# A step's output rows, four to a partition: the output product's stationary operand taken at every fourth column

## The chip, the cores and the metric

The kernel runs on one core of a Trainium2 chip. The metric is the device time of one execution, in microseconds; three executions of the kernel before are given, and one more was profiled. Five engines of the core appear below: PE does matmuls (PEld is its loading of the stationary operand, shown apart), DVE, ACT and POOL do elementwise work, SP issues transfers. ACT issues transfers as well; a q behind an engine's name (ACTq, SPq) means its queue of such issues.

## What is computed

A channel attention is followed by a gated convolution, for 4 batches of 6,336 rows and 256 channels:

```python
qn = q / (np.linalg.norm(q, axis=1, keepdims=True) + 1e-06)
kn = k / (np.linalg.norm(k, axis=1, keepdims=True) + 1e-06)
s = kn.transpose(0, 2, 1) @ qn / tau            # 256 x 256 per batch
a = softmax(s, axis=-1)
x = v @ a                                       # 6336 x 256 per batch
gate = sigmoid(causal convolution of x over 5 rows, one filter per channel)
out = (gate * (x @ w_val)) @ w_out
```

All inputs and the output are float32, apart from the three weights, which come as float64.

## The kernel before

The scores `s` need all rows of a batch, so a batch has two phases, and the second phase of one batch runs beside the first of the next. In the first, `score_group` takes three rows per partition of q and k, splits part of them into a high and a low half (`hi` holds both) and multiplies them on PE into `s_ps` (L235). There the stationary operand is dealt: every second column, so that channels c and c + 1 fall into two halves. In the second, each batch is cut into 13 steps, twelve of 508 rows and a last one of 240. Of each step `load_v` and `transpose_v` bring v with channels on the partitions, `conv` makes the convolved gate (`x_ps`, L378, then DVE's and ACT's work from L395 on), `value` multiplies it with `val_ps`, and `split_g` splits the result into `g_hi` and `g_lo` (two halves of 128 channels, the step's rows along each partition).

`finish`, which the change rewrites, does the last product. It cuts the step's 508 rows into `nt` = 4 tiles of 128 (the last starts at row 380, so it overlaps the third by 4 rows); a tile is the stationary operand, 128 neighbouring columns of `g_hi` or `g_lo`, and the moving operand is 256 columns of `wo_hi` or `wo_lo`:

```python
nc.tensor.matmul(o_ps[:, u * C:(u + 1) * C], gs[:, h, off:off + P], ws[:, h, :], ...)
```

Two halves of channels times three products (high by high, high by low, low by high) give six matmuls per tile and 24 per step. Two tiles share a bank `o_ps`, which ACT copies in one piece into `o_sb` (L455). `o_sb` has two buffers in turn, so a step's copy waits until the store of two steps earlier has landed. Then ACT issues two stores: three tiles of 128 partitions (L460, 384 KB in pieces of 1 KB) and the remaining 124 rows from partitions 4 to 127 (L462, 124 KB). The step before the last stores from SP. In the very last step (240 rows, two tiles) ACT copies one tile and stores it, DVE copies the other and SP stores it (L451, L453).

The order of work on each engine is settled when the program is built: the main loop writes out turns of score groups, softmax pieces and the parts of a step, with priorities (`end`) and with `behind`, which holds a part back until a marked instruction has been placed. `marks["ACT"]` in `finish` is such a mark. `raw_p` is the pool of the q and k tiles (tag `raw`, six buffers), `w_p` that of `gate`, `g_hi`, `g_lo` and `o_sb`.

Of the kernel before, what the change touches and what calls it, by code (L numbers as in the profile page):

```python
# [9 lines left out]
F32 = mybir.dt.float32  # L10
# [8 lines left out]
P = 128  # L19
# [11 lines left out]
def kernel(  # L31
# [13 lines left out]
    nc = tc.nc  # L45
    B, N, C = q.shape
# [6 lines left out]
    raw_p = ctx.enter_context(tc.tile_pool(name="raw_p", bufs=6))  # L53
# [5 lines left out]
    w_p = ctx.enter_context(tc.tile_pool(name="w_p", bufs=2))  # L59
# [5 lines left out]
    first = RP % GROUP or GROUP  # L65
# [267 lines left out]
    NT = -(-(HALO + WMAX) // P)  # L333
# [83 lines left out]
    def split_g(b, i):  # L417
# [11 lines left out]
            nc.gpsimd.tensor_tensor(gl[:, :, 0:w], gate[:, :, 0:w], gh[:, :, 0:w].bitcast(F32), ALU.subtract)  # L429
        gts[b, i] = (gh, gl)  # L430

    def finish(b, i):
        t0, w = chunks[i]
        gh, gl = gts.pop((b, i))
        nt = -(-w // P)
        offs = [min(j * P, w - P) for j in range(nt)]
        o_sb = w_p.tile([P, NT, C], F32, name="o_sb")
        for j in range(0, nt, 2):
            pair = offs[j:j + 2]
            o_ps = ps.tile([P, 512], F32, name="o_ps", tag="bank")  # L440
            for u, off in enumerate(pair):
                n_ = 0
                for h in range(NH):
                    for gs, ws in ((gh, wo_hi), (gh, wo_lo), (gl, wo_hi)):
                        nc.tensor.matmul(o_ps[:, u * C:(u + 1) * C], gs[:, h, off:off + P], ws[:, h, :],  # L445
                                         start=n_ == 0, stop=n_ == 3 * NH - 1)
                        n_ += 1
            if (b, i) == all_steps[-1]:

                for u, (copy, dma) in enumerate(((nc.scalar.copy, nc.scalar), (nc.vector.tensor_copy, nc.sync))[:len(pair)]):  # L450
                    copy(o_sb[:, j + u, :], o_ps[:, u * C:(u + 1) * C])  # L451
                    first = max((j + u) * P - pair[u], 0)
                    dma.dma_start(out=out[b, t0 + pair[u] + first:t0 + pair[u] + P], in_=o_sb[first:P, j + u, :])  # L453
                continue
            marks["ACT"] = nc.scalar.copy(o_sb[:, j:j + len(pair), :], o_ps[:, 0:len(pair) * C].rearrange("p (j c) -> p j c", c=C))  # L455
        if (b, i) == all_steps[-1]:
            return
        full = w // P
        store = nc.sync if (b, i) == all_steps[-2] else nc.scalar
        store.dma_start(out=out[b, t0:t0 + full * P].rearrange("(j p) c -> p j c", p=P), in_=o_sb[:, 0:full, :])  # L460
        if w % P:
            store.dma_start(out=out[b, t0 + full * P:t0 + w], in_=o_sb[P - w % P:P, full, :])  # L462


    all_groups = [(b, g) for b in range(B) for g in range(NG)]
    all_steps = [(b, i) for b in range(B) for i in range(NC)]
# [5 lines left out]
    marks = {}  # L472
# [106 lines left out]
    for n in range(len(all_steps)):  # L579
# [38 lines left out]
        if prev:  # L618
            with behind(*{len(all_steps) - 2: ["CONV"], len(all_steps) - 1: ["G"]}.get(n, [])):
                finish(*prev)  # L620
    finish(*all_steps[-1])


# [30 lines left out]
```

## Time and profile before

| | |
|---|---|
| median of 3 executions | 617.93 us (617.14 to 620.77) |
| profiled execution, its own time | 619.46 us |
| its span, first to last instruction | 617.7 us |
| mean granted TensorE clock in it | 0.995 |
| moved by transfers | 105.80 MB in 154,596 packets, 171 GB/s |
| read from and written to memory | 79.16 MB, 25.95 MB |

The span is what the stretches and the chain add up to; the execution's own time has 1.76 us more around it. In rows of the trace, `out<-in` are the program's names for the tiles, `x20` is a count, and L445 is a line of the kernel. Rows of a tile give durations as least/median/greatest in ns; rows of groups give busy us and mean ns behind the first bar, and idle time with what ended it behind the second; rows of waits give us in total, times, and the longest. In a timeline the bracket holds the idle time ahead of a row and what ended it. A busy PE is not PE at its peak, since matmuls overlap in the pipeline and their ends are modelled: the distance from one start to the next is the better measure.

### The profile page before, as it was taken

The numbers are of one execution on the slowest core, as the hardware profiler recorded it, in microseconds if no ns is written. First come the engines' busy times: TensorE is split into PE (matmuls) and PEld (weight loads), VectorE is DVE, ScalarE is ACT, GpSimd is POOL, SyncE is SP. The second block draws the span as 40 slices with busy tenths as digits, with TensorE's granted clock in tenths as the row PEclk, the third lists the DMA queues.
The fourth block names the chain that finished last, engine by engine and source line by source line (L and its number), as shares of the span: only waits on it lengthen the run. The fifth ranks groups of instructions, "written<-read, shape, count | busy, mean of one in ns | idle before, by whom it ended". The sixth has DMA issues, their size and how long they took to land.

```text
span 617.7 us, 10242 instructions
## 1 busy us (share of the span) xinstructions
PE 598.4 (97%) x3596; PEld 536.2 (87%) x3596; DVE 497.8 (81%) x763; ACT 469.9 (76%) x576; POOL 489.7 (79%) x261
## 2 busy tenths in 40 slices
PE   8998798999999999999999999999999899999995
PEld 7997597888988999999899899898998788888895
DVE  3785687888887979888977887988887888988782
ACT  5566775869789887787878987887877876877763
POOL 2692699889987599899995799998986485887842
PEclk9999999999999999999999999999999999999998
DMA  8989979465566566665564757665143254552113
GB/s 274 401 288 249 315 226 224 137 184 175 177 186 188 152 187 199 186 180 161 184 186 125 220 174 204 176 197 135 52 118 86 69 128 127 131 142 83 63 51 110
DMA packets 154596, 105.80 MB, mean 171 GB/s; under 512 B 110768, under 2 KB 137648, under 8 KB 154544
## 3 DMA queue, kind: packets, MB, share of 16 engines
q1 hardware_dynamic: 128768, 79.82, 45.7%
q10 hardware_dynamic: 25776, 25.32, 13.5%
q8 instruction: 28, 0.46, 0.3%
q14 instruction: 24, 0.20, 0.1%
HBM read 79.16 MB, written 25.95 MB: 170 GB/s over the span
## 4 chain that ended last, share of the span: by engine, by line
PE 78%; DMA 6%; ACT 4%; issue 4%; POOL 3%; DVE 2%; SPq 2%; ACTq 0%; DVEq 0%; POOLq 0%
PE s_ps L235 20%; PE o_ps L445 19%; PE x_ps L378 18%; PE val_ps L378 18%; DMA v_raw<-in_v_dram 4%; SPq L358 1%; POOL hi L201 1%; DMA out_dram<-o_sb 1%; POOL v_lo L368 1%; PE o_ps L321 1%; DMA raw<-in_q_dram 1%; DVE gate L398 1%; PE s_ps L241 1%; DVE gate L415 1%; ACT v_hi L367 0%
## 5 line engine op out<-in xcount | busy, mean ns | idle before, releaser
L398 DVE SCALAR_TENSOR_TENSOR gate<-x_ps,wa,gate 128x508 f32<-128x508 f32 (+1 forms) x400 | 268.2, 715 | 17.8 <-ACT gate L395 15.2
L201 POOL TENSOR_TENSOR hi<-raw,hi 128x1536 fp32r<-128x1536 f32 (+3 forms) x51 | 141.9, 2783 | 21.2 <-ACT hi L200 20.4
L368 POOL TENSOR_TENSOR v_lo<-v_raw,v_hi 128x1024 fp32r<-128x1024 f32 (+1 forms) x52 | 123.0, 2367 | 39.4 <-ACT v_hi L367 32.7
L378 PE MATMUL x_ps<-v_hi,w 128*128 128x512 f32 (+1 forms) x416 | 140.8, 389 | 0.9 <-DVE gate L398 0.9
L378 PE MATMUL val_ps<-v_hi,w 128*128 128x508 f32 (+1 forms) x416 | 135.5, 386 | 2.7 <-DVE w L326 2.1
L429 POOL TENSOR_TENSOR g_lo<-gate,g_hi 128x1016 fp32r<-128x1016 f32 (+1 forms) x50 | 118.2, 2364 | 21.3 <-ACT g_hi L428 21.0
L445 PE MATMUL o_ps<-wo_hi,g_hi 128*128 128x256 f32 x400 | 113.1, 286 | 0.3 <-ACT g_hi L428 0.3
L445 PE MATMUL o_ps<-wo_lo,g_hi 128*128 128x256 f32 x400 | 111.2, 281 | 0.0
L222 DVE TENSOR_TENSOR acc_ps<-acc_ps,sq 128x512 f32<-128x512 f32 (+1 forms) x124 | 85.7, 691 | 29.4 <-ACT sq L217 26.0
L217 ACT ACTIVATE sq<-raw 128x1536 f32<-128x1536 f32 (+3 forms) x69 | 96.0, 1395 | 15.5 <-DMA raw<-in_k_dram 8.3
L445 PE MATMUL o_ps<-wo_hi,g_lo 128*128 128x256 f32 x400 | 107.5, 282 | 0.0
L222 POOL TENSOR_TENSOR acc<-acc,sq 128x512 f32<-128x512 f32 x68 | 88.1, 1295 | 22.1 <-ACT sq L217 16.4
L235 PE MATMUL s_ps<-hi 128*128 128x256 f32 (+1 forms) x714 | 97.7, 286 | 2.0 <-POOL hi L201 2.0
L235 PEld LDWEIGHTS s_ps<-hi 128*128 128x128 f32 (+1 forms) x714 | 91.8, 195 | 4.6 <-POOL hi L201 2.7
L366 DVE STREAM_TRANSPOSE v_raw<-v_raw 128x1024 f32<-128x1024 f32 (+1 forms) x52 | 62.4, 1201 | 40.9 <-DMA v_raw<-in_v_dram 33.9
L378 PEld LDWEIGHTS val_ps<-v_hi,w 128*128 128x128 f32 x416 | 77.8, 190 | 17.4 <-DVE w L326 2.5
L378 PEld LDWEIGHTS x_ps<-v_hi,w 128*128 128x128 f32 x416 | 77.1, 188 | 14.9 <-PE s_ps L235 1.3
L395 ACT ACTIVATE gate<-x_ps,wa 128x508 f32<-128x508 f32 (+1 forms) x104 | 68.1, 666 | 20.6 <-PE x_ps L378 19.7
L378 PE MATMUL x_ps<-v_lo,w 128*128 128x512 f32 (+1 forms) x208 | 79.7, 383 | 0.0
L378 PE MATMUL val_ps<-v_lo,w 128*128 128x508 f32 (+1 forms) x208 | 79.4, 382 | 0.0
L445 PEld LDWEIGHTS o_ps<-wo_hi,g_hi 128*128 128x128 f32 x400 | 75.2, 188 | 4.5 <-ACT g_hi L428 0.7
L235 PE MATMUL s_ps<-raw 128*128 128x256 f32 (+1 forms) x324 | 77.0, 383 | 1.2 <-DMA raw<-in_k_dram 1.2
(81 smaller groups left out, 799.2 us busy)
## 6 DMA issues: line engine op xcount, KB each, us to landing
raw<-in_q_dram SPq DMA_DIRECT2D x64, 384.0 KB
raw<-in_k_dram SPq DMA_DIRECT2D x64, 384.0 KB
v_raw<-in_v_dram SPq DMA_DIRECT2D x176, 128.0 KB
out_dram<-o_sb ACTq DMA_DIRECT2D x47, 384.0 KB
out_dram<-o_sb ACTq DMA_DIRECT2D x47, 124.0 KB
v_raw<-in_v_dram SPq DMA_DIRECT2D x16, 120.0 KB
v_raw<-in_v_dram SPq DMA_DIRECT2D x16, 64.0 KB
raw<-in_q_dram SPq DMA_DIRECT2D x4, 128.0 KB
```

What stands on the lines that cost most here:

```text
L201: nc.gpsimd.tensor_tensor(hi[r, js, :, 1, :], raw[r, js, :, :], hi[r, js, :, 0, :].bitcast(F32), ALU.subtract)
L217: nc.scalar.activation(sq[0:np_, ja:jb], raw[0:np_, ja:jb], AF.Square)
L222: add = eng.tensor_tensor(st[key][0:np_], st[key][0:np_], sq[0:np_, j], ALU.add)
L235: marks["PE"] = nc.tensor.matmul(st["s"][:, h, :], lhs, rhs, start=False, stop=stop and h == NH - 1 and n_ == len(ops) - 1)
L241: nc.tensor.matmul(st["s"].rearrange("p h c -> p (h c)"), zeros[:, 0:P], zeros, start=False, stop=False)
L366: nc.vector.transpose(t, t)
L368: nc.gpsimd.tensor_tensor(tl[:, :, 0:g, :], t, th[:, :, 0:g, :].bitcast(F32), ALU.subtract)
L378: marks["PRODUCT"] = nc.tensor.matmul(ps, wt[:, which, ws, ch, hs], vs[:, ch, lo:hi_], start=n_ == 0, stop=n_ == 3 * NH - 1)
L395: nc.scalar.activation(gate[:, h, 0:w], x_ps[:, 0:w], AF.Copy, scale=cw[:, h, 0:1])
L398: nc.vector.scalar_tensor_tensor(gate[:, h, 0:w], x_ps[:, tap:tap + w], cw[:, h, tap:tap + 1], gate[:, h, 0:w], ALU.mult, ALU.add)
L429: nc.gpsimd.tensor_tensor(gl[:, :, 0:w], gate[:, :, 0:w], gh[:, :, 0:w].bitcast(F32), ALU.subtract)
L445: nc.tensor.matmul(o_ps[:, u * C:(u + 1) * C], gs[:, h, off:off + P], ws[:, h, :], start=n_ == 0, stop=n_ == 3 * NH - 1)
```

## The change

A step's rows are dealt out differently: row 4r + j goes to partition r of tile j, where row 128j + r did before. So a tile has 127 rows (508 / 4) instead of 128, its stationary operand is every fourth column of `g_hi` or `g_lo`, and after the two copies partition r of `o_sb` holds rows 4r to 4r + 3, 4 KB that lie together in the output. The last step of a batch has 240 rows in two tiles: 120 rows each, every second column.

```diff
+    def even(rows):
+        whole_ = rows // 16 * 16
+        return [x for x in ((0, whole_), (whole_, rows)) if x[0] < x[1]]
...
-        offs = [min(j * P, w - P) for j in range(nt)]
-        o_sb = w_p.tile([P, NT, C], F32, name="o_sb")
+        rows = w // nt
+        at_end = (b, i) == all_steps[-1]
+        if not at_end:
+            o_sb = w_p.tile([P, NT, C], F32, name="o_sb")
...
-                        nc.tensor.matmul(o_ps[:, u * C:(u + 1) * C], gs[:, h, off:off + P], ws[:, h, :],
+                        turn = gs[:, h, 0:w].rearrange("p (r j) -> p j r", j=nt)[:, j + u, :]
+                        nc.tensor.matmul(o_ps[0:rows, u * C:(u + 1) * C], turn, ws[:, h, :],
...
+            dst = out[b, t0:t0 + w].rearrange("(r j) c -> r j c", j=nt)
...
-                    copy(o_sb[:, j + u, :], o_ps[:, u * C:(u + 1) * C])
-                    first = max((j + u) * P - pair[u], 0)
-                    dma.dma_start(out=out[b, t0 + pair[u] + first:t0 + pair[u] + P], in_=o_sb[first:P, j + u, :])
+                    o_end = raw_p.tile([P, C], F32, name="o_end", tag="raw")
+                    copy(o_end[0:rows], o_ps[0:rows, u * C:(u + 1) * C])
+                    for r0, r1 in even(rows):
+                        dma.dma_start(out=dst[r0:r1, j + u, :], in_=o_end[r0:r1])
...
-        store.dma_start(out=out[b, t0:t0 + full * P].rearrange("(j p) c -> p j c", p=P), in_=o_sb[:, 0:full, :])
-        if w % P:
-            store.dma_start(out=out[b, t0 + full * P:t0 + w], in_=o_sb[P - w % P:P, full, :])
+        for r0, r1 in even(rows):
+            store.dma_start(out=dst[r0:r1], in_=o_sb[r0:r1, 0:nt, :])
```

The stores are cut at a multiple of 16 partitions: 112 and 15 for a full step, 112 and 8 for the last. In the program's very last step the two copies go to tiles `o_end` of the q and k pool instead of `o_sb`, and each is stored in two pieces.

The order of the instructions stays. On PE, in the middle of the program (the end of one step's `finish`, score products of the next batch, the next step's value product), the rows before are

```order
L445 MATMUL o_ps<-wo_hi,g_hi 128x256
L445 MATMUL o_ps<-wo_lo,g_hi 128x256
L445 MATMUL o_ps<-wo_hi,g_lo 128x256
L235 MATMUL s_ps<-hi 128x256 x18
L378 MATMUL val_ps<-v_hi,w 128x508
```

and now

```order
L453 MATMUL o_ps<-wo_hi,g_hi 127x256
L453 MATMUL o_ps<-wo_lo,g_hi 127x256
L453 MATMUL o_ps<-wo_hi,g_lo 127x256
L235 MATMUL s_ps<-hi 128x256 x18
L378 MATMUL val_ps<-v_hi,w 128x508
```

Nothing moved; an output tile has 127 rows for 128. On ACT, at the end of the program (the stores of the step two before the last, the copies of the step before the last, and the last step; DMAHW names are the transfers waited for), the rows before are

```order
L460 DMA out_dram<-o_sb 128x3x256 [waits Activation_49]
L462 DMA out_dram<-o_sb 124x256
L455 COPY o_sb<-o_ps 128x512 [waits DMAHW6_49,DMAHW5_49,PE_49]
L455 COPY o_sb<-o_ps 128x512 [waits PE_49]
L451 COPY o_sb<-o_ps 128x256 [waits DMAHW7_49,DMAHW0_49,PE_49]
L453 DMA out_dram<-o_sb 128x256 [waits Activation_49]
```

and now

```order
L471 DMA out_dram<-o_sb 15x1024
L465 COPY o_sb<-o_ps 127x512 [waits DMAHW6_49,DMAHW5_49,PE_49]
L465 COPY o_sb<-o_ps 127x512 [waits PE_49]
L461 COPY o_end<-o_ps 120x256 [waits PE_49]
L463 DMA out_dram<-o_end 112x256 [waits Activation_49]
L463 DMA out_dram<-o_end 8x256
```

The last copy no longer waits for transfers, and one store became two; DVE's last copy waits for ACT's in both programs.

More of the change, by code (lines that the diff above doesn't have):

```diff
@@ L435, in finish @@
         nt = -(-w // P)
-        offs = [min(j * P, w - P) for j in range(nt)]
-        o_sb = w_p.tile([P, NT, C], F32, name="o_sb")
+        rows = w // nt
+        at_end = (b, i) == all_steps[-1]
+        if not at_end:
+            o_sb = w_p.tile([P, NT, C], F32, name="o_sb")
         for j in range(0, nt, 2):
-            pair = offs[j:j + 2]
+            pair = range(j, min(j + 2, nt))
             o_ps = ps.tile([P, 512], F32, name="o_ps", tag="bank")
-            for u, off in enumerate(pair):
+            for u in range(len(pair)):
                 n_ = 0
@@ L444, in finish @@
                     for gs, ws in ((gh, wo_hi), (gh, wo_lo), (gl, wo_hi)):
-                        nc.tensor.matmul(o_ps[:, u * C:(u + 1) * C], gs[:, h, off:off + P], ws[:, h, :],
+                        turn = gs[:, h, 0:w].rearrange("p (r j) -> p j r", j=nt)[:, j + u, :]
+                        nc.tensor.matmul(o_ps[0:rows, u * C:(u + 1) * C], turn, ws[:, h, :],
                                          start=n_ == 0, stop=n_ == 3 * NH - 1)
                         n_ += 1
-            if (b, i) == all_steps[-1]:
+            dst = out[b, t0:t0 + w].rearrange("(r j) c -> r j c", j=nt)
+            if at_end:
                 for u, (copy, dma) in enumerate(((nc.scalar.copy, nc.scalar), (nc.vector.tensor_copy, nc.sync))[:len(pair)]):
-                    copy(o_sb[:, j + u, :], o_ps[:, u * C:(u + 1) * C])
-                    first = max((j + u) * P - pair[u], 0)
-                    dma.dma_start(out=out[b, t0 + pair[u] + first:t0 + pair[u] + P], in_=o_sb[first:P, j + u, :])
+                    o_end = raw_p.tile([P, C], F32, name="o_end", tag="raw")
+                    copy(o_end[0:rows], o_ps[0:rows, u * C:(u + 1) * C])
+                    for r0, r1 in even(rows):
+                        dma.dma_start(out=dst[r0:r1, j + u, :], in_=o_end[r0:r1])
                 continue
-            marks["ACT"] = nc.scalar.copy(o_sb[:, j:j + len(pair), :], o_ps[:, 0:len(pair) * C].rearrange("p (j c) -> p j c", c=C))
-        if (b, i) == all_steps[-1]:
+            marks["ACT"] = nc.scalar.copy(o_sb[0:rows, j:j + len(pair), :],
+                                          o_ps[0:rows, 0:len(pair) * C].rearrange("p (j c) -> p j c", c=C))
+        if at_end:
             return
-        full = w // P
         store = nc.sync if (b, i) == all_steps[-2] else nc.scalar
-        store.dma_start(out=out[b, t0:t0 + full * P].rearrange("(j p) c -> p j c", p=P), in_=o_sb[:, 0:full, :])
-        if w % P:
-            store.dma_start(out=out[b, t0 + full * P:t0 + w], in_=o_sb[P - w % P:P, full, :])
+        for r0, r1 in even(rows):
+            store.dma_start(out=dst[r0:r1], in_=o_sb[r0:r1, 0:nt, :])
     all_groups = [(b, g) for b in range(B) for g in range(NG)]
```

## The prediction, made before the changed kernel ran

> **What bounds the kernel now.** I read the page's busy shares first, then busy time by stretches, then the chain of waits inside a full stretch, then the timeline of single loads.
>
> ```profile
> PE 598.4 (97%) x3596; PEld 536.2 (87%) x3596; DVE 497.8 (81%) x763; ACT 469.9 (76%) x576; POOL 489.7 (79%) x261
> ```
> ```profile
> core 0: us, PE busy (x) PEld busy (x) DVE busy (x) ACT busy (x) POOL busy (x), PEclk, DMA share, GB/s
> ...
> 95.00:200.00 105.00, 101.73 (x625) 90.56 (x625) 86.58 (x129) 83.74 (x100) 93.76 (x48) 1.00 0.65 179
> 200.00:450.00 250.00, 250.00 (x1590) 227.45 (x1589) 214.15 (x328) 205.07 (x243) 224.71 (x107) 1.00 0.59 169
> 450.00:500.00 50.00, 48.26 (x292) 43.00 (x292) 41.85 (x66) 39.57 (x56) 33.24 (x21) 1.00 0.40 104
> 500.00:611.00 111.00, 111.00 (x677) 99.21 (x676) 89.51 (x134) 78.57 (x111) 76.20 (x40) 1.00 0.36 99
> 611.00:617.70 6.70, 0.42 (x4) 0.22 (x2) 0.42 (x1) 0.37 (x1) 0.00 (x0) 0.75 0.40 130
> ```
>
> From 95 us, where the first output is stored, to 611 us PE is without work for 3.27 us (105.00 - 101.73) and 1.74 us (50.00 - 48.26), and for nothing in the other 361 us. So what a matmul of this part takes from start to start is time of the kernel, one to one, and what DVE, ACT or a transfer gains there is worth 5.0 us at most. The durations that the profile gives for matmuls overlap; the pace is read from bursts in the chain of waits (start us, us, what):
>
> ```profile
> 367.70 2.35 PE o_ps L445 x20
> 370.05 2.16 PE s_ps L235 x18
> 372.21 2.73 PE val_ps L378 x12
> ...
> 377.31 2.76 PE x_ps L378 x12
> ```
>
> Start to start that is 117.5 ns for o_ps (2.35/20), 120 ns for s_ps (2.16/18), 227.5 ns for val_ps with 508 moving columns, 230 ns for x_ps with 512. What stands between two o_ps matmuls shows in the timeline:
>
> ```profile
> 302.08 0.28 PE L445 MATMUL o_ps<-wo_hi,g_hi 128*128 128x256 f32 x1
> 302.08 0.19 PEld L445 LDWEIGHTS o_ps<-wo_lo,g_hi 128*128 128x128 f32 x1
> 302.20 0.28 PE L445 MATMUL o_ps<-wo_lo,g_hi 128*128 128x256 f32 x1
> ```
>
> The load for the next matmul starts when this matmul starts, and the next matmul follows 0.12 us later. One load per matmul, each beside one stream of 256 columns: if the load grows beyond about 118 ns, the pace of o_ps grows with it, and nothing hides that.
>
> **The stationary operand at every fourth column.** This is the large term. No row of this trace has a step of four; it has step one and step two.
>
> ```profile
> L445 PEld LDWEIGHTS o_ps<-wo_hi,g_hi x400: 186/188/193, 88.2 to 610.8; 128*128 128x128 f32 x134
> L267 PEld LDWEIGHTS o_ps<-ones,acc_all x32: 186/194/198, 53.2 to 471.6; 128*128 128x128 f32 x32
> ```
> ```profile
> L235 PEld LDWEIGHTS s_ps<-hi x714: 189/195/201, 46.6 to 472.9; 128*128 128x128 f32 x175, 64*128 64x128 f32 x4
> ```
> ```profile
> 53.18 0.99 PEld L267 LDWEIGHTS o_ps<-ones,acc_all 128*128 128x128 f32 x8 [0.33 <-issue]
> ```
> ```profile
> L367 ACT CAST v_hi<-v_raw 128x1024 fp32r<-128x1024 f32 x48 | 54.4, 1135 | 10.9 <-PE val_ps L378 7.0 <-DVE v_raw L366 2.2 <-DMA v_raw<-in_v_dram 1.4
> ...
> L200 ACT CAST hi<-raw 128x1024 fp32r<-128x1024 f32 x22 | 23.3, 1058 | 0.0
> ```
>
> L445 reads neighbouring columns (188 ns), L235 every second one (195 ns); L267 does both on one tile (186 to 198). ACT pays as little for a step of two: 1135 ns for 1,024 elements against 1058. The eight loads of L267, with one moving column each, have only themselves to wait for: (0.99 - 0.19)/7 = 114 ns apart. So a load holds its path for about 114 ns already, as long as the 256 columns take.
>
> The lower end is that the step costs nothing or as much as a step of two: 0 to 2.5 ns a matmul (120 - 117.5). A price for each column that is skipped (one at step two, three at step four) gives 7.5 ns. The upper end comes from the bytes that an operand spans in its partition. 256 contiguous columns are 1,024 B and take 117.5 ns; 508 are 2,032 B and take 227.5 ns. The stationary operand of s_ps spans 1,024 B, takes 120 ns, and is just dearer than one of 512 B: as if a read went at some 2,032 B in 227.5 ns whatever it picks out, 114 ns for 1,024 B and, by proportion, 57 ns for 512 B, where the load's own 114 ns ends last. That one rate fits the four paces and the small extra at step two. The new operand has 127 columns over 507 x 4 + 4 = 2,032 B: 227.5 ns, plus the 2.5 ns that s_ps shows over o_ps, so 230 ns. I take this end, because it explains rows that a price per column leaves unexplained (why 256 columns need 117.5 ns and 512 need 230).
>
> [...]
>
> How many loads pay: 4 batches x 12 full steps x 4 tiles x 6 products = 1,152 at step four. (The 48 of the four last steps have a step of two and 120 columns: 0.1 us.) By the order of PE, which the change leaves as it is, 86 of the 1,200 stand behind a matmul of 508 or 512 columns, whose 227.5 to 230 ns hide the longer load. 1,152 - 86 = 1,066 pay 230 - 117.5 = 112.5 ns: 119.9 us. PE idles for 5.0 us in the part concerned, waiting for other engines that now get more time; I take half back: -2.5 us. One row fewer (127 for 128) saves nothing on 256 moving columns.
>
> **Stores of 112 and 15 partitions.** The number of issues per step stays two; the last step has four instead of two.
>
> ```profile
> L460 ACTq DMA_DIRECT2D out_dram<-o_sb x50: 351/383/437, 94.9 to 608.1; - x50
> ```
> ```profile
> q10 hardware_dynamic: 25776, 25.32, 13.5%
> ```
> ```profile
> DVE v_raw L366 <- DMA v_raw<-in_v_dram: 33.9, 24, 3.0
> ...
> ACT gate L408 <- DMA out_dram<-o_sb: 3.0, 1, 3.0
> ...
> ACT o_sb L451 <- DMA out_dram<-o_sb: 2.0, 1, 2.0
> ```
>
> 25,776 packets become about a quarter as many if a partition's 4 KB go as one. That may shorten the 13.5% of the queue's time and let v_raw land sooner, but DVE's 33.9 us of waiting lie beside a full PE, and the 3.0 us of ACT are among the 5.0 us. Inside 0 and -5.0 us I take 0, since the slower PE covers these waits anyway; the copies of 127 rows cost what 128 did.
>
> **The last copies.** They now write tiles of their own in the pool of q and k, free since the last score group.
>
> ```profile
> 608.48 4.13 DMA out_dram<-o_sb
> ```
> ```profile
> 611.14 0.28 PE L445 MATMUL o_ps<-wo_hi,g_lo 128*128 128x256 f32 x1
> 612.67 0.37 ACT L451 COPY o_sb<-o_ps 128x256 f32<-128x256 f32 x1 [2.04 <-DMA out_dram<-o_sb]
> 613.07 0.35 ACTq L453 DMA_DIRECT2D out_dram<-o_sb  x1
> 613.08 0.42 DVE L451 COPY o_sb<-o_ps 128x256 f32<-128x256 f32 x1 [4.31 <-ACT o_sb L451]
> 613.53 0.32 SPq L453 DMA_DIRECT2D out_dram<-o_sb  x1
> ```
>
> ACT's copy waits until the store of two steps earlier has landed (608.48 + 4.13 = 612.61), though its matmuls end at 611.42. Without that wait the copy starts 1.2 us earlier; DVE's still stands behind ACT's, by its wait. SP then issues two stores, so a second 0.32 us comes on top: -1.2 + 0.3 = -0.9 us. The landing of the last one (617.70 - 613.85 = 3.85 us with the program's end) stays. If the larger store ahead of it fills the queue, the gain is 0; if the small last store lands sooner, it is some 2 us.
>
> **Sum.** The profiled execution took 619.46 us (span 617.70 and 1.76 around it): 619.46 + 119.9 + 0.1 - 2.5 - 0.9 = 736.1 us. The median of the runs shown lies 1.53 us below that execution; against it I say 735 us.
>
> **Rivals.**
> 1. The step is nearly free (not slower): the load's path is paced by columns, and step two's 7 ns are all there is. For it: 188 against 195 ns, 1058 against 1135. Against it: the one rate above. At 0 to 2.5 ns for 1,152 loads: 617.93 - 0.9 + (0 to 2.9) = 617.0 to 619.9 us; at 7.5 ns, 625.7. It decides below about 6 ns a load (7.1 us / 1,152), where the result stays within 1%. Chance 0.24.
> 2. A partial price: the load reads ahead while the matmul before it streams, and gets half longer, 1.5 x 114 = 171 ns. 1,066 x 53.5 ns = 57 us, so 674 us. For it speaks only that neither end is shown. Chance 0.15.
> 3. Faster: loads cost nothing, and the shorter stores take away PE's 5.0 us of idling and 1 to 2 us at the end: 611 to 612 us. Against it: most of the 33.9 us of waiting touch nothing. Chance 0.05.
> The forecast has the remaining 0.56.
>
> **How the numbers follow.** About 1%, or 6.2 us, is what a measurement of this kernel can tell from no change. The forecast and rival 2 are slower (0.71), and the dear end of rival 1 adds 0.03: 0.74. The rest of rival 1 with a little of rival 3 is within 1%: 0.22. Faster: 0.04. The forecast's own range is 715 to 748 us (idle taken back wholly or not at all, a load between 215 and 242 ns). To hold 8 in 10 the range must reach to rival 1, so it runs from 618 to 748; below lie the free end of rival 1 and rival 3, some 0.13, above 0.04.
>
> **What would show it.** In the profile after, the loads of o_ps should take about 188 + 116 = 304 ns instead of 188, bursts of o_ps some 230 ns a matmul, those of s_ps, x_ps and val_ps what they take now. PE should have almost no idle time after 95 us, and the wait of the last copy for a store should be gone. If loads read 190 to 200 ns and bursts 118 to 125 ns, the reasoning on bytes is wrong and rival 1 holds. If o_ps bursts are as slow but the time grew much less than 100 us, PE was not as full as I read it. If the granted clock, 1.00 in these stretches, falls because the array streams less, it is worse than I say.

## The result, and the profile after

The changed kernel takes 734.31 us (median of 6 executions, 733.73 to 735.99), the kernel before 619.72 us beside it (6 executions, 617.14 to 621.73). The ratio is 1.186, with a 95% interval of 1.182 to 1.189: slower by 114.6 us. The profiled execution took 735.99 us, its span is 734.2 us, against 619.46 and 617.7 before.

The page after, busy shares of the engines and the queue of the stores:

```profile
PE 719.3 (98%) x3596; PEld 661.5 (90%) x3596; DVE 504.1 (69%) x763; ACT 474.9 (65%) x576; POOL 489.4 (67%) x261
...
q10 hardware_dynamic: 8002, 25.32, 11.0%
```

PE has the same 3,596 matmuls and is busy for 120.9 us more; loads (PEld) are busy for 125.3 us more. DVE, ACT and POOL do the same work as before (504, 475 and 489 us against 498, 470 and 490), spread over a longer time. The packets of the stores fell from 25,776 to 8,002.

Busy time by stretches after, with the same columns as the table before:

```profile
95.00:200.00 105.00, 103.41 (x531) 95.39 (x531) 75.71 (x109) 66.16 (x75) 81.78 (x40) 1.00 0.59 158
200.00:450.00 250.00, 249.33 (x1314) 231.20 (x1313) 178.12 (x273) 178.44 (x217) 183.49 (x89) 1.00 0.52 149
450.00:500.00 50.00, 50.00 (x257) 46.70 (x257) 35.42 (x51) 31.93 (x35) 35.71 (x17) 1.00 0.48 138
500.00:611.00 111.00, 110.40 (x552) 101.85 (x551) 79.61 (x120) 73.52 (x98) 68.93 (x39) 1.00 0.31 81
611.00:728.00 117.00, 117.00 (x533) 108.84 (x532) 69.27 (x104) 62.12 (x86) 59.55 (x31) 1.00 0.25 70
```

From 95 to 728 us PE is full but for 1.59 + 0.67 + 0.60 = 2.86 us (5.01 us from 95 to 611 us before), with a granted clock of 1.00 in all five stretches. In the 250 us from 200 on it does 1,314 matmuls where it did 1,590. So the time went into the pace of matmuls, not into waiting and not into the clock. Which matmuls, the chain of waits after tells (start us, us, what):

```profile
112.47 4.53 PE o_ps L453 x20
117.00 2.73 PE val_ps L378 x12
...
130.64 2.15 PE s_ps L235 x18
...
177.21 2.77 PE x_ps L378 x12
```

Twenty o_ps matmuls take 4.53 us where they took 2.35. The others stand: val_ps 2.73 (2.73 before), s_ps 2.15 (2.16), x_ps 2.77 (2.76). The tile view after shows whose load grew (least/median/greatest ns):

```profile
L453 PEld LDWEIGHTS o_ps<-wo_hi,g_hi x400: 186/328/335, 87.7 to 729.1; 128*127 128x127 f32 x128, 128*120 128x120 f32 x6
...
L235 PEld LDWEIGHTS s_ps<-hi x714: 189/195/220, 46.2 to 552.3; 128*128 128x128 f32 x175, 64*128 64x128 f32 x4
```

The load at every fourth column takes 328 ns for 188, the one at every second column 195 as before. The loads of the four last steps, with a step of two and 120 columns, stay short (188 to 190 ns in the mean). One burst in the timeline after, from the value product before it to the convolution behind it (rows of PE and PEld alone):

```profile
366.84 0.39 PE L378 MATMUL val_ps<-v_hi,w 128*128 128x508 f32 x1
366.84 0.31 PEld L453 LDWEIGHTS o_ps<-wo_hi,g_hi 128*127 128x127 f32 x1
367.07 0.29 PE L453 MATMUL o_ps<-wo_hi,g_hi 128*127 128x256 f32 x1
367.07 0.31 PEld L453 LDWEIGHTS o_ps<-wo_lo,g_hi 128*127 128x127 f32 x1
367.19 0.39 PE L453 MATMUL o_ps<-wo_lo,g_hi 128*127 128x256 f32 x1
367.28 0.33 PEld L453 LDWEIGHTS o_ps<-wo_hi,g_lo 128*127 128x127 f32 x1
367.42 0.39 PE L453 MATMUL o_ps<-wo_hi,g_lo 128*127 128x256 f32 x1
...
367.89 0.40 PE L453 MATMUL o_ps<-wo_lo,g_hi 128*127 128x256 f32 x1
367.99 0.21 PEld L378 LDWEIGHTS x_ps<-v_hi,w 128*128 128x128 f32 x1
368.12 0.39 PE L378 MATMUL x_ps<-v_hi,w 128*128 128x512 f32 x1
```

The first load lies beside the long val_ps matmul and costs nothing (366.84 to 367.07 is the pace of 508 columns). The second matmul follows after 0.12 us; from there each comes 0.23 us after the last, 367.19 to 367.42, and so does the x_ps matmul behind the burst (367.89 to 368.12). So a burst of n pays n - 1 times, as the count of 86 hidden loads has it. In numbers: (4.53 - 0.118)/19 = 232 ns, and 1,066 x (232 - 118) = 121.5 us. With 2.15 us of idle time taken back and an end that is 1.77 us shorter (below) that makes 117.6 us; the spans differ by 116.5, so about 1 us is unaccounted for.

### The profile page after: what moved, and what is told of

The parts are those of the page before. It is cut to its first block, busy times and chain, and to the rows that moved or that the text cites. A ratio compares the mean times of both kernels' runs of the same rounds, so it can differ in the third digit from the quotient of the medians.

```text
span 734.2 us, 10240 instructions
## 1 busy us (share of the span) xinstructions
PE 719.3 (98%) x3596; PEld 661.5 (90%) x3596; DVE 504.1 (69%) x763; ACT 474.9 (65%) x576; POOL 489.4 (67%) x261
## 4 chain that ended last, share of the span: by engine, by line
PE 90%; DMA 4%; ACT 2%; DVE 1%; SPq 1%; issue 1%; POOL 0%; DVEq 0%; ACTq 0%; POOLq 0%
PE o_ps L453 36%; PE x_ps L378 18%; PE s_ps L235 18%; PE val_ps L378 17%; DMA v_raw<-in_v_dram 2%; DMA raw<-in_q_dram 2%; PE o_ps L321 1%; DMA out_dram<-o_sb 1%; SPq L358 1%; DMA raw<-in_k_dram 1%; PE s_ps L241 1%; POOL hi L201 0%; PE o_ps L267 0%; DVE v_raw L366 0%; ACT hi L200 0%
## 5 line engine op out<-in xcount | busy, mean ns | idle before, releaser
L453 PE MATMUL o_ps<-wo_lo,g_hi 128*127 128x256 f32 (+1 forms) x400 | 156.4, 391 | 0.0
L453 PE MATMUL o_ps<-wo_hi,g_hi 128*127 128x256 f32 (+1 forms) x400 | 152.5, 381 | 0.3 <-ACT g_hi L428 0.3
L453 PE MATMUL o_ps<-wo_hi,g_lo 128*127 128x256 f32 (+1 forms) x400 | 147.4, 382 | 0.0
L465 ACT COPY o_sb<-o_ps 127x512 f32<-127x512 f32 (+1 forms) x99 | 58.1, 587 | 127.4 <-PE o_ps L453 127.1
L453 PEld LDWEIGHTS o_ps<-wo_hi,g_hi 128*127 128x127 f32 (+1 forms) x400 | 127.3, 318 | 3.2 <-ACT g_hi L428 0.7
L453 PEld LDWEIGHTS o_ps<-wo_lo,g_hi 128*127 128x127 f32 (+1 forms) x400 | 128.1, 320 | 0.2
L453 PEld LDWEIGHTS o_ps<-wo_hi,g_lo 128*127 128x127 f32 (+1 forms) x400 | 125.2, 321 | 1.4
L415 DVE TENSOR_TENSOR gate<-val_ps,gate 128x508 f32<-128x508 f32 (+1 forms) x104 | 65.7, 657 | 54.6 <-PE val_ps L378 31.5
```

What stands on the lines that cost most here:

```text
L415: nc.vector.tensor_tensor(gate[:, h, 0:w], val_ps[:, 0:w], gate[:, h, 0:w], ALU.mult)
L453: nc.tensor.matmul(o_ps[0:rows, u * C:(u + 1) * C], turn, ws[:, h, :], start=n_ == 0, stop=n_ == 3 * NH - 1)
L465: marks["ACT"] = nc.scalar.copy(o_sb[0:rows, j:j + len(pair), :], o_ps[0:rows, 0:len(pair) * C].rearrange("p (j c) -> p j c", c=C))
```

## The experiments

Two theories go in. The prediction's: an operand is read at a fixed rate over all the bytes that it spans in its partition (bytes spanned). Its rival: each element costs by how many elements share one small piece of memory, so that the price stops growing once every element stands alone (accesses). In both, twice the time at step four; they part elsewhere. Unless said otherwise, an edit is on the changed kernel. The diffs are cut: dots mark what is left out, and where only new lines stand, the lines that they replace are left out too.

**The step alone undone.** Everything else of the change stays: 127 rows a tile, 112 and 15 partitions, last copies in the pool of q and k. A tile is 127 neighbouring columns again, so the stores go in pieces of 1 KB again.

```diff
-                        turn = gs[:, h, 0:w].rearrange("p (r j) -> p j r", j=nt)[:, j + u, :]
+                        turn = gs[:, h, (j + u) * rows:(j + u + 1) * rows]
...
-            dst = out[b, t0:t0 + w].rearrange("(r j) c -> r j c", j=nt)
+            dst = out[b, t0:t0 + w].rearrange("(j r) c -> r j c", j=nt)
```

> The changed kernel with one thing put back: a tile's stationary operand is 127 neighbouring columns again (rows 127j to 127j + 126), the stores of 112 and 15 partitions write pieces of 1 KB, the last copies stay in the pool of q and k. Theory (the step of four alone lengthens the load): loads of o_ps 188 ns, bursts 117 to 118 ns a matmul, about 619 us, 0 to 2 us below before. Rival (127 columns instead of 128, or the stores): loads stay near 328 ns, or the time stays above 700 us.

Measured: 619.88 us against 620.62, ratio 0.9998 (0.9973 to 1.0023). Its o_ps loads in the tile view:

```profile
L453 PEld LDWEIGHTS o_ps<-wo_hi,g_hi x400: 180/187/195, 87.3 to 613.5; 128*127 128x127 f32 x128, 128*120 128x120 f32 x6
```

187 ns again, and a burst of 20 takes 2.37 us. The loss is gone with the step. The 4 KB pieces went with it, so this run alone can't tell the two apart; the kernel under "Dealing elsewhere" keeps the pieces and is 1.1% slower, not 18.6%. The parts that stay (127 rows, the cut of the stores at 112 partitions, the last copies) together move nothing that this run can tell. The same kernel was timed once more, with more rounds, beside the last experiment:

> The run with 127 neighbouring columns once more, beside the one that has only the last copies, on the same chip: its tail was 4.53 us. Theory (the stores of 112 and 15 partitions gain nothing beside a full PE): the same as the last copies alone within 0.3%, 0 to 2 us below before. Rival (the shorter stores gain in the middle of the program): more than 2 us below the run with the last copies alone.

619.86 us against 621.55, ratio 0.9984 (0.9963 to 1.0005). The gain of some 1.8 us that the end of the trace shows (below) would be 0.3% and is inside that interval.

**A step of two.** Rows dealt two to a partition, twice: stores in pieces of 2 KB, loads at every second column.

```diff
+                        turn = gs[:, h, 0:w].rearrange("p (i r j) -> p i j r", j=2, r=rows)[:, (j + u) // 2, (j + u) % 2, :]
...
+            dst = out[b, t0:t0 + w].rearrange("(i r j) c -> r i j c", j=2, r=rows)
...
```

> Rows dealt two to a partition: every second column of each half of the step, pieces of 2 KB. Theory (a read goes at a fixed rate over the bytes that it spans, 1,016 B here): loads about 195 ns, bursts 120 ns as in s_ps, 619.7 - 0.9 + 1,152 x 2.5 ns = 621.7 us. Rival (any step breaks a fast way of loading): loads near 328 ns, about 734 us.

Measured: 621.07 us against 620.62, ratio 1.0005 (0.9977 to 1.0033).

```profile
L453 PEld LDWEIGHTS o_ps<-wo_hi,g_hi x400: 186/194/202, 89.7 to 616.2; 128*127 128x127 f32 x128, 128*120 128x120 f32 x6
```

194 ns, like s_ps, and 2.40 us for 20. Step two is free in this kernel, by both theories. It also doubles the size of the stores' pieces (2 KB for the 1 KB of the first experiment), and nothing comes of that.

**A step of three.** The product then reads other columns than its rows ask for.

```diff
+                        turn = gs[:, h, j + u:j + u + 3 * (rows - 1) + 1:3] if nt == 4 else gs[:, h, 0:w].rearrange("p (r j) -> p j r", j=nt)[:, j + u, :]
```

> Every third column of a step, 127 of them (an output row is another row's, and the columns past 381 go unused); the stores are those of the changed kernel. Theory by bytes (1,516 B spanned): interval 170 + 2.5 = 172 ns, 619.7 + 1,066 x 54.5 ns = 677 us. [...] Rival (cost per skipped column, so a third of the way from step two to four is missing): interval 120 + 56 = 176 ns, hardly to be told from the first.

Measured: 677.19 us, ratio 1.091 (1.087 to 1.096).

```profile
L453 PEld LDWEIGHTS o_ps<-wo_hi,g_hi x400: 185/260/267, 88.9 to 671.6; 128*127 128x127 f32 x128, 128*120 128x120 f32 x6
```

260 ns, and bursts of 20 take 3.45 us: (3.45 - 0.118)/19 = 175 ns. The price rises evenly between step two (120) and step four (232); it isn't a switch between two modes. A price for each column skipped, 176 ns here, fits as well as 172 ns by bytes; the next experiment parts them from the count of accesses.

**A step of eight.** Each tile takes every eighth column over both halves of `g_hi` or `g_lo`, so that it spans 4,036 B instead of 2,020.

```diff
+                        turn = gs.rearrange("p h w -> p (h w)")[:, j + u:j + u + 8 * (rows - 1) + 1:8] if nt == 4 else gs[:, h, 0:w].rearrange("p (r j) -> p j r", j=nt)[:, j + u, :]
```

> Every eighth column over both halves of channels of a tile in a row, 127 columns over 4,036 B (the product is of other numbers than the reference's). Theory by bytes, as in the prediction: interval 452 + 2.5 = 455 ns, 1,066 x 337 ns + 86 x 225 ns = 379 us more, about 998 us. Rival by accesses (one access for each element as soon as none share 16 bytes, whatever lies between): loads 328 ns and interval 232 ns as for a step of four, about 734 us.

Measured: 746.17 us, ratio 1.202 (1.198 to 1.207).

```profile
L453 PEld LDWEIGHTS o_ps<-wo_hi,g_hi x400: 185/336/343, 88.5 to 738.6; 128*127 128x127 f32 x128, 128*120 128x120 f32 x6
```

336 ns, and 4.68 us for 20. (4.68 - 0.118)/19 = 240 ns a matmul. The rival by accesses, which asks for what step four took (columns 16 bytes apart: 328 ns, 232 ns), is 8 ns short of both. The reading by bytes spanned, which asks for some 250 us more, falls here: twice the span costs 8 ns a load more than step four. So does a price for each skipped column, seven here and three at step four. What lies between the elements costs those 8 ns and no more.

**The moving operand at a step of two.** As the first experiment (stationary operand contiguous), with 256 weights taken at every second place; the weights are then the wrong ones for the columns.

```diff
+                        turn = gs[:, h, (j + u) * rows:(j + u + 1) * rows]
+                        nc.tensor.matmul(o_ps[0:rows, u * C:(u + 1) * C], turn, ws.rearrange("p h e -> p (h e)").rearrange("p (e t) -> p t e", t=2)[:, h, :],
```

> As the run with 127 neighbouring stationary columns, but the moving operand is every second column of both halves of the output weights in a row: 256 columns over 2,048 B (the product is of other weights than the reference's). Theory of the prediction (moving and stationary operands are read alike, at 2,032 B in 227.5 ns, so that the 117.5 ns of 256 contiguous columns are the time of their 1,024 B): 230 ns a matmul, 1,200 x 112 ns = 135 us more, about 754 us. Rival (the moving operand is paced by its columns, and the agreement with 508 columns was a coincidence): 118 to 120 ns a matmul, about 620 us; then the longer load is a matter of the loading path alone.

Measured: 748.96 us against 621.67, ratio 1.205 (1.202 to 1.208). The tile view and, in a second fence, the chain of waits:

```profile
L453 PEld LDWEIGHTS o_ps<-wo_hi,g_hi x400: 181/207/214, 89.8 to 742.8; 128*127 128x127 f32 x128, 128*120 128x120 f32 x6
L453 PE MATMUL o_ps<-wo_hi,g_hi x400: 387/409/577, 89.9 to 743.0; 128*127 128x256 f32 x128, 128*120 128x256 f32 x6
```
```profile
689.13 4.60 PE o_ps L453 x20
```

Now the loads are short (207 ns) and the matmuls are long: 4.60/20 = 230 ns for 256 moving columns, as much as 512 contiguous ones take. At this step, the only one tried, the moving operand goes at the rate of the stationary one (232 ns for 127 columns at step four), and it pays in full: 230 ns for the 117.5 that 256 contiguous columns take from one matmul to the next. (Bytes and accesses ask for the same here.)

**Dealing elsewhere.** The rows are dealt while `g_hi` and `g_lo` are written: ACT and POOL read `gate` at every fourth element and write contiguous tiles, PE reads neighbouring columns, and the stores keep their 4 KB pieces.

```diff
-        gate = gates.pop((b, i))
+        nt = -(-w // P)
+        dealt_g = gates.pop((b, i))[:, :, 0:w].rearrange("p h (r j) -> p h j r", j=nt)
...
-            nc.scalar.copy(gh[:, :, 0:w], gate[:, :, 0:w])
-            nc.gpsimd.tensor_tensor(gl[:, :, 0:w], gate[:, :, 0:w], gh[:, :, 0:w].bitcast(F32), ALU.subtract)
+            ghj, glj = (t[:, :, 0:w].rearrange("p h (j r) -> p h j r", j=nt) for t in (gh, gl))
+            nc.scalar.copy(ghj, dealt_g)
+            nc.gpsimd.tensor_tensor(glj, dealt_g, ghj.bitcast(F32), ALU.subtract)
...
```

> The rows are dealt out earlier: ACT's cast and POOL's subtraction in the split read the gate at every fourth column and write the halves tile by tile, so the stationary operand is 127 neighbouring columns again, while the stores keep their pieces of 4 KB. The order of instructions shifts a little. Theory (on PE the step costs because PE has no slack; ACT and POOL have some): loads of o_ps 188 ns, bursts 118 ns. If ACT pays one access of about 1.8 ns an element as PE's load does, its cast takes about 2.0 us instead of 1.05, 50 us more on an engine that is busy for 470 of 618; POOL, whose pace a step of two does not touch, perhaps 2.4 to 3.5 us instead of 2.36. Time 620 to 632 us. Rival (the dearer cast is on the path from the gate to the output product, and PE waits for it): PE idle for over 15 us, time above 640 us.

Measured: 628.93 us against 621.67, ratio 1.011 (1.009 to 1.014). Groups of this kernel, with shapes kept apart (busy us, mean ns, idle time before):

```profile
L432 POOL TENSOR_TENSOR g_lo<-gate,g_hi 128x1016 fp32r<-128x1016 f32 x47 | 138.4, 2945 | 32.7 <-ACT g_hi L431 32.7
...
L431 ACT CAST g_hi<-gate 128x1016 fp32r<-128x1016 f32 x47 | 97.5, 2075 | 21.7 <-DVE gate L415 21.0 <-DVE gate L398 0.4
```

and the same two of the kernel before:

```profile
L429 POOL TENSOR_TENSOR g_lo<-gate,g_hi 128x1016 fp32r<-128x1016 f32 x47 | 114.5, 2435 | 21.3 <-ACT g_hi L428 21.0 <-DMA raw<-in_k_dram 0.4
...
L428 ACT CAST g_hi<-gate 128x1016 fp32r<-128x1016 f32 x47 | 49.2, 1048 | 23.1 <-DVE gate L415 22.8 <-ACT gate L395 0.2
```

ACT's copy doubles, 1048 to 2075 ns, and POOL's takes 510 ns more. The stretch of this kernel that was full of matmuls before:

```profile
200.00:450.00 250.00, 245.83 (x1551) 222.97 (x1552) 208.98 (x319) 220.61 (x242) 229.31 (x104) 1.00 0.60 170
```

PE's bursts are back to 2.37 us for 20, but in these 250 us it is idle for 4.2 us where it was never idle, and does 1,551 matmuls for 1,590. ACT and POOL are busy for 221 and 229 of the 250 us. From 95 to 611 us PE is idle for 10.1 us (5.0 before). What it waits for, over the whole run:

```profile
PE x_ps L378 <- DVE gate L398: 2.5, 4, 1.1
PE s_ps L235 <- POOL hi L201: 2.4, 1, 2.4
...
PE o_ps L456 <- ACT o_sb L468: 1.7, 2, 1.5
PE o_ps L456 <- ACT g_hi L431: 1.7, 2, 1.1
```

For `g_hi` it waits 1.7 us (0.3 before), for `g_lo` never; the larger part is for other work, `gate`, `hi` and the copies of `o_ps`, which comes later. That the two dearer copies push all of it back is argued, not shown: no run has one of them without the other. The price is far smaller than on PE, yet it is a price, and the 4 KB pieces don't earn it back.

**The last copies alone.** On the kernel before: only the very last copies go to tiles of their own, the stores stay as they were.

```diff
-        o_sb = w_p.tile([P, NT, C], F32, name="o_sb")
+        if (b, i) != all_steps[-1]:
+            o_sb = w_p.tile([P, NT, C], F32, name="o_sb")
...
-                    copy(o_sb[:, j + u, :], o_ps[:, u * C:(u + 1) * C])
+                    o_end = raw_p.tile([P, C], F32, name="o_end", tag="raw")
+                    copy(o_end, o_ps[:, u * C:(u + 1) * C])
...
```

> The kernel before with the last copies alone changed: they write tiles of the q and k pool, everything else (tiles of 128 neighbouring columns, stores of 128 and 124 partitions) stays. Theory (the copy's wait for a store is all that the change gains): from the end of the last matmul to the end of the span 4.5 to 5.0 us instead of 6.27, so 1.3 to 1.7 us or 0.2 to 0.3% off the time, at the edge of what five rounds tell. Rival (without the shorter stores the last store queues behind the 124-partition one and lands as late as before): 6.0 to 6.3 us at the end, no change in the time.

Measured: 621.18 us against 621.55, ratio 0.9995 (0.9972 to 1.0018). SP's issues at its end, in the timeline, and after them those of the changed kernel:

```profile
614.15 0.41 SPq L462 DMA_DIRECT2D out_dram<-o_sb  x1
614.61 0.43 SPq L464 DMA_DIRECT2D out_dram<-o_sb  x1
615.81 0.33 SPq L455 DMA_DIRECT2D out_dram<-o_end  x1
```
```profile
728.91 0.82 SPq L471 DMA_DIRECT2D out_dram<-o_sb  x2
730.58 0.73 SPq L463 DMA_DIRECT2D out_dram<-o_end  x2
```

The last matmul ends at 614.92 us here, at 729.69 after and at 611.42 before. From there to the end of the last issue, and from that to the end of the span:

| kernel | to the last issue's end | from there to the span's end | both |
|---|---|---|---|
| before | 613.85 - 611.42 = 2.43 us | 617.70 - 613.85 = 3.85 us | 6.28 us |
| last copies alone | 616.14 - 614.92 = 1.22 us | 621.9 - 616.14 = 5.76 us | 6.98 us |
| after | 731.31 - 729.69 = 1.62 us | 734.2 - 731.31 = 2.89 us | 4.51 us |

The issue comes 1.2 us sooner, as worked out, and the landing gives it all back: SP has issued the store of 124 partitions (L464) 1.2 us ahead of it, and the last one lands later behind that. Here 45 GB/s still move in the 3.3 us from 618.1 us on, 2.0 us behind the last issue; in the changed kernel 227 GB/s move in the 1.3 us from the last issue on, and 1 GB/s in the 1.6 us behind them. Only together with the stores cut at 112 partitions is the end shorter: 3.75 to 4.62 us in the traces of all six other kernels above that have these stores, whether their pieces have 1, 2 or 4 KB. The last store itself has 112 partitions in this kernel too (and 8 more rows in a store of their own in the changed one), so the difference is put down to the 124 partitions ahead of it; no run changed that store alone.

## Why the prediction was right, point by point

**PE is full, so its pace is the time.** Right. 2.86 us of idle time from 95 to 728 us, and the spans differ by what 1,066 matmuls pay, less what the idle time and the end give back, to about 1 us.

**The size of the pace.** 230 ns was forecast, 232 measured: 121.5 us for 119.9. The reason was right in what it needed for step four and wrong beyond it. (By its own terms, idle time taken back wholly or not at all and 215 to 242 ns, the forecast's range comes to 716 to 750 us, not 715 to 748; the result lies in the middle of both. And a tile of 127 columns spans 2,020 B, not 2,032, which would take 1.3 ns off a load.) The runs give one table; the pieces are those of 16 bytes that 127 elements touch when laid on a grid:

| step | 16-byte pieces | load, ns | 20 matmuls, us | time, us |
|---|---|---|---|---|
| 1 | 32 | 187 | 2.37 | 619.9 |
| 2 | 64 | 194 | 2.40 | 621.1 |
| 3 | 95 | 260 | 3.45 | 677.2 |
| 4 | 127 | 328 | 4.53 | 734.3 |
| 8 | 127 | 336 | 4.68 | 746.2 |

The rate that the prediction read from contiguous operands, 2,032 B in 227.5 ns, is 1.8 ns for each 16 bytes. Up to step four, bytes spanned and pieces touched are the same number, which is why the wrong reading gave the right forecast. It was luck that step four is the largest step at which they agree. At step eight the span doubles and the pieces don't: 998 us was what the bytes asked for, 746 is what came. The moving operand fits too: 256 columns at step two touch 128 pieces, 128 x 1.8 = 230 ns, measured 230. In these runs stationary and moving pieces don't add up, the larger count sets the pace: step two has 64 of each and still takes 120 ns. That a piece has 16 bytes is an estimate from where the price stops growing, between step three (12 bytes from one element to the next, 175 ns) and step eight (32 bytes, 240): at step four, 16 bytes, it is nearly all there (232). No run has a step between four and eight, and the grid is not shown otherwise. The extra 8 ns of step eight over step four are not explained.

**The load's own time.** The term was mis-sized. 188 + 116 = 304 ns was forecast, 328 measured. The record grew by 140 ns where the pace grew by 114; why the two differ is open, and since the pace is what counts, the sum doesn't feel it.

**86 loads hidden behind long matmuls.** Right, by the timeline above: the first load of a burst costs nothing.

**Idle time taken back.** 2.15 us for the forecast 2.5, between the ends of 0 and 5.0.

**The stores in the middle, taken at nothing.** Right, as far as a full PE can show it. In the waits after:

```profile
DVE v_raw L366 <- DMA v_raw<-in_v_dram: 5.9, 7, 1.8
...
ACT w L325 <- DMA out_dram<-o_sb: 1.0, 1, 1.0
```

DVE's wait for v_raw fell from 33.9 to 5.9 us and ACT's waits for stores from 5.0 to 1.0 us. Much of that is only the longer time in which the same bytes move: with PE at its old pace v_raw is waited for 18.8 us in the first experiment, with pieces of 1 KB. Nothing of it reaches PE there: its idle time from 95 to 611 us is 7.3 us, 5.0 before. Pieces of 4 KB beside the old pace and undealt copies were not run.

**The last copies.** The term was mis-sized, and its reason was half of it: -0.9 us forecast, -1.77 measured (6.28 to 4.51 us). The step that failed is "the landing of the last one ... stays". The wait is gone and the issue comes 0.8 us sooner in the changed kernel (2.43 to 1.62 us), but by itself, as the last experiment shows, that gains nothing; the other 0.96 us are the landing, 3.85 to 2.89. The prediction named both ends: a gain of 0 because of the larger store ahead (the last copies alone, 6.98 us), or a last store that lands sooner and some 2 us (the changed kernel).

**The rivals.** That the step is nearly free falls with the 232 ns, and holds for step two (120); the load is not paced by its columns alone, since 127 of them took 187 to 336 ns. The partial price, 674 us, is not what step four costs; it is what step three costs (677), and the table puts that down to 95 pieces touched for 127, not to a load that reads ahead. That the shorter stores make the kernel faster finds no support: without the dear loads, 619.88 against 620.62 with pieces of 1 KB, 621.07 with 2 KB, and 628.93 against 621.67 with 4 KB, where ACT and POOL pay for the dealing.

## What to carry to other kernels

On a full PE, count for each matmul the pieces (16 bytes by the estimate above) that its stationary and its moving operand touch in a partition, and compare the larger count with the length of the stream: here, with operands of 4 bytes an element, each piece took 1.8 to 1.9 ns; beside 256 moving columns a stationary operand of 127 columns took a step of two almost for nothing (120 ns a matmul for 118), and a moving operand did not (230). The layout that was to help the stores was paid here by whoever read across it, PE most (18.6%), ACT and POOL less (1.1%), and the larger pieces of the stores gave nothing back that a run could tell. And look at what stands ahead of the last transfer: with the store of 124 partitions there, issuing the last one 1.2 us sooner made this end no shorter (6.98 us for 6.28).

## What the runs showed of the hardware that was not expected

- The price of a step saturates: step eight (336 ns a load) costs hardly more than step four (328 ns).
- The moving operand is not free at a step of two: 256 columns take 230 ns a matmul there, as 512 contiguous ones do, and 117.5 ns side by side.
- ACT pays little at a step of two and double at a step of four: 1058 to 1135 ns for 1,024 elements, but 1048 to 2075 ns for 1,016. POOL, with one of two operands at step four, goes from 2435 to 2945 ns.
- With the moving operand at a step of two, the contiguous stationary loads take 207 ns for 187; why is open.
